# Attention ahead of two expert layers: plain float32 matmuls in place of split ones in the first 16 head units

## The chip, the cores and the metric
The kernel runs on one core of a Trainium2 chip. The core has TensorE for matmuls (the profile lists its weight loads as PEld beside PE), VectorE (DVE), ScalarE (ACT), GpSimd (POOL) and SyncE (SP), whose queue issues the DMAs here. The metric is the device time of one execution in microseconds; lower is better.

## The reference
Causal attention with a bias goes over 4 batches of 8 heads, 576 positions and 64 channels; its output feeds a gated layer and that one a second layer.

```python
scores = scale * np.matmul(q, k.transpose(0, 1, 3, 2))
cum = np.cumsum(np.maximum(s, 0.0), axis=-1)
bias = -(cum[:, :, :, None] - cum[:, :, None, :])
scores = np.where(causal, -1000000000.0, scores + np.minimum(bias, 0.0))
scores = scores - np.max(scores, axis=-1, keepdims=True)
attn = np.exp(scores)
attn = attn / (np.sum(attn, axis=-1, keepdims=True) + 1e-09)
out = np.matmul(attn, v)
# x: (2304, 512)
x = (1.0 / (1.0 + np.exp(-(x @ w_gate))) * (x @ w_val)) @ w_out
h = x @ w_in
y = (h - np.tanh(h)) @ w_out2
```

The weights and inputs are float32; w_gate and w_val are 512 by 1536.

## The kernel before
Matmuls use a reduced float32 type (called R in the code, fp32r in the profile). To keep float32 accuracy, each operand is split into a high part (a copy into R by ScalarE) and a low part (the difference, by GpSimd or VectorE), and products of the parts are summed in PSUM.

The attention works in head units of one batch, one head and one half G of the queries. The order is all units with G = 0 (queries 0 to 255, query tiles t = 0 and 1), 32 of them, and then those with G = 1 (tiles 2, 3, 4). Each unit has one step per tile, so the first 16 units are steps 0 to 31. An iteration i of the main loop handles several steps at once, as a pipeline written out by hand: `ttr(i)` adds scores and the broadcast cumulative sum and takes the row extreme (VectorE, L345); `exp(i)` is on ScalarE (L352); `eps`, `recip` and `norm` of step i-1 divide by the sum (VectorE, L356, L361, L370); `qk(i+1)` computes scores on TensorE (L331, L332); `tr(i-1)` transposes the probabilities through TensorE (L382); `evac(i-2)` copies them out of PSUM as high part (ScalarE, L395) and low part (VectorE, L396); `pv` multiplies by v when a unit's last tile is through (L409). `xsum` adds the two halves of the result (ScalarE copy L424, VectorE add L425), and `xsplit` splits the attention output of a pair of heads into high and low (ScalarE L433, GpSimd L434). Every engine runs its instructions in the order in which the code emits them.

For the scores, q is stored with its high part on partitions 0 to 63 and its low part on 64 to 127 (the input holds q and k twice, one below the other), so one matmul against the high part of k and one against its low part give all four products. `split_kq` makes these parts (ScalarE L284 and L288, GpSimd L285 and L289) and `split_v` those of v (ScalarE L302, GpSimd L303).

Loads are issued by SP in program order: `load_kq` two to three units ahead (L256), `load_vc` two units ahead (the broadcast rows of the cumulative sum, L268, and v, L270). Beside the attention, `Conversion.tick` prepares the 24 weight blocks of the gated layer, of 512 KB raw each, in three stages that overlap over ticks: a scaling on ScalarE (L74), a join on VectorE (L78, L79), the split (ScalarE L108, GpSimd L109). Three raw blocks are in flight; each tick issues the next load (L95). Two ticks (PRE) come ahead of the loop, then one in the iterations of `CS` (1, 3, ..., 13), then one in each from 15 on. When the eight heads of a batch and half are through, the loop hands out 24 groups of twelve expert matmuls each (`moe`, L456 to L460), two an iteration; the first are in iteration 20. The results go to DRAM (L442), and the two later stages follow after the attention.

Where the words end the code goes on:

Of the kernel before, what the change touches and what calls it, by code (L numbers as in the profile page):

```python
# [8 lines left out]
F = mybir.dt.float32  # L9
R = mybir.dt.float32r  # L10
U = mybir.dt.uint32
AF = mybir.ActivationFunctionType
ALU = mybir.AluOpType

B, H, S, D = 4, 8, 576, 64
# [11 lines left out]
NSP = 3  # L27
NK = 3
KA = 2
PRE = 2  # L30
CS = (1, 3, 5, 7, 9, 11, 13)
RAW0 = 2
AHEAD = 1
TR2 = 16
MP = M2 // 2
# [11 lines left out]
def width(t):  # L47
    return Q0[t] + 128
# [11 lines left out]
def attention_moe_moe2(ctx: ExitStack, tc: tile.TileContext, kqT, v, s, wg, wv, wo, win, wo2, out):  # L60
    nc = tc.nc
    PE, ACT, DVE, POOL, SP = nc.tensor, nc.scalar, nc.vector, nc.gpsimd, nc.sync
# [6 lines left out]
    def bank(i, shape):  # L69
        return psum.tile(shape, F, tag=f"bank{i}", name=f"bank{i}")  # L70
# [158 lines left out]
    ld = a_right.enter_context(tc.tile_pool(name="ld", bufs=2, side="right"))  # L229
    at = a_right.enter_context(tc.tile_pool(name="at", bufs=2, side="right"))  # L230
# [3 lines left out]
    make_identity(nc, ident)  # L234
    NPT = 1
    pts = [[pt.tile([128, 5, 320], R, name=f"pt{p}{i}") for p in "hl"] for i in range(NPT)]
    for st in pts:
        for p in st:
            POOL.memset(p.bitcast(F), 0.0)

    units = [(b, G, h) for G in range(2) for b in range(B) for h in range(H)]
    steps = [(u, t) for u, (b, G, h) in enumerate(units) for t in GRP[G][2]]
    U_ = {}

    def shape(u):
        b, G, h = units[u]
        q0, qw, ts = GRP[G]
        return b, h, q0, q0 + qw, qw, 2 if G == 0 else 5

    def load_kq(u):  # L250
        if u >= len(units):
            return
        b, h, q0, kw, qw, nj = shape(u)
        d = U_[u] = {}
        kq = ld.tile([128, S + 320], F, tag="kq", name="kq")[:, :kw + qw]
        SP.dma_start(out=kq, in_=kqT[b, h, :, 0:512] if q0 == 0 else kqT[b, h, :, 256:1152])  # L256
        d["q"], d["k"] = (kq[:, 0:256], kq[:, 256:512]) if q0 == 0 else (kq[:, S:], kq[:, :S])

    def load_vc(u):
        if u >= len(units):  # L260
            return
        b, h, q0, kw, qw, nj = shape(u)
        d = U_[u]
        d["v"] = ld.tile([128, 5, D], F, tag="v", name="vraw")[:, :nj]
        d["c"] = c = ld.tile([128, CW], F, tag="c", name="cbc", bufs=3)
        for t in GRP[units[u][1]][2]:
            k0 = 288 if t == 4 else 0
            SP.dma_start(out=c[:, CO[t]:CO[t] + width(t) - k0],  # L268
                         in_=cscr[b * H + h, k0:width(t)].partition_broadcast(128))
        SP.dma_start(out=d["v"], in_=v[b, h, :, 0:nj])  # L270

    parts, vparts = [], []

    def split_kq(u):
        if u >= len(units):
            return
        b, h, q0, kw, qw, nj = shape(u)
        d = U_[u]
        d["kh"] = kh = at.tile([128, S], R, tag="kh", name="kh", bufs=NK)[:, :kw]
        d["kl"] = kl = at.tile([128, S], R, tag="kl", name="kl", bufs=NK)[:, :kw]  # L280
        d["qs"] = qs = at.tile([128, 320], R, tag="qs", name="qs", bufs=NK)[:, :qw]

        def part_k():
            ACT.activation(out=kh, in_=d["k"], func=AF.Copy)  # L284
            POOL.tensor_tensor(out=kl, in0=d["k"], in1=kh.bitcast(F), op=ALU.subtract)  # L285

        def part_q():
            ACT.activation(out=qs, in_=d["q"], func=AF.Copy)  # L288
            POOL.tensor_tensor(out=qs[64:128], in0=d["q"][64:128], in1=qs[64:128].bitcast(F), op=ALU.subtract)  # L289

        parts.extend([part_k, part_q])

    def split_v(u):
        if u >= len(units):
            return
        b, h, q0, kw, qw, nj = shape(u)
        d = U_[u]
        d["vs"] = vs = at.tile([128, 5, 2, D], R, tag="vs", name="vs")[:, :nj]
        a = h % 2

        def part_v():
            ACT.activation(out=vs[:, :, a, :], in_=d["v"], func=AF.Copy)  # L302
            POOL.tensor_tensor(out=vs[:, :, 1 - a, :], in0=d["v"], in1=vs[:, :, a, :].bitcast(F), op=ALU.subtract)  # L303

        vparts.append(part_v)

    T_ = {}
    nqk = [0]
# [9 lines left out]
    def qk(i):  # L318
        if i >= len(steps):
            return  # L320
        u, t = steps[i]
        d = U_[u]
        q0 = GRP[units[u][1]][0]
        o = Q0[t] - q0
        w = width(t)
        cuts = [(0, max(w, 256))] if t < 4 else [(0, 288), (288, 576)]
        T_[i] = {"qk": []}
        for c0, c1 in cuts:
            ps = bank(3 + nqk[0] % 3, [128, c1 - c0])
            nqk[0] += 1  # L330
            PE.matmul(ps, d["qs"][:, o:o + 128], d["kh"][:, c0:c1], start=True, stop=False)  # L331
            PE.matmul(ps, d["qs"][:, o:o + 128], d["kl"][:, c0:c1], start=False, stop=True)  # L332
            T_[i]["qk"].append((ps, c0, min(c1, w)))
# [51 lines left out]
    def evac(i):  # L385
        if i < 0 or i >= len(steps):
            return
        u, t = steps[i]
        G = units[u][1]
        e = T_.pop(i)  # L390
        n = e["n"]
        ph, pl = pts[u % NPT]
        o = Q0[t] - GRP[G][0] + (64 if t == 4 else 0)
        js = slice(0, t + 1) if G else slice(0, 3 * t + 1, 3)
        ACT.activation(out=ph[:, js, o:o + n], in_=e["tr"], func=AF.Copy)  # L395
        DVE.tensor_tensor(out=pl[:, js, o:o + n], in0=e["tr"], in1=ph[:, js, o:o + n].bitcast(F), op=ALU.subtract)  # L396

    X_ = {}

    def pv(u):  # L400
        b, G, h = units[u]
        q0, qw, ts = GRP[G]
        d = U_.pop(u)
        ph, pl = pts[u % NPT]
        ps = bank(7, [128, qw])
        jobs = [(0, 0, 0), (1, 3, 0)] if G == 0 else [(0, 0, 0), (1, 1, 0), (2, 2, 0), (3, 3, 64), (4, 4, 64)]
        for n, (j, slot, o) in enumerate(jobs):
            for m, p in enumerate((ph, pl)):
                PE.matmul(ps[:, o:qw], d["vs"][:, j].rearrange("p a d -> p (a d)"), p[:, slot, o:qw],  # L409
                          start=(n == 0 and m == 0), stop=(n == len(jobs) - 1 and m == 1))  # L410
        return ps

    def xsum(u, ps):
        b, G, h = units[u]
        q0, qw, ts = GRP[G]
        g = 2 * b + G
        if h == 0:
            X_[g] = [xt.tile([128, KD, 320], R, tag=f"x{p}", name=f"x{p}")[:, :, :qw] for p in "hl"]
        a = 64 * (h % 2)
        if h % 2 == 0:  # L420
            X_["pair"] = at.tile([128, 320], F, tag="xp", name="xp", bufs=1)[:, :qw]
        xp = X_["pair"]
        tmp = at.tile([128, 320], F, tag="xtmp", name="xtmp", bufs=1)[:, :qw]
        ACT.activation(out=tmp[a:a + 64], in_=ps[64 - a:128 - a], func=AF.Copy)  # L424
        DVE.tensor_tensor(out=xp[a:a + 64], in0=ps[a:a + 64], in1=tmp[a:a + 64], op=ALU.add)  # L425

    def xsplit(u):
        b, G, h = units[u]
        g = 2 * b + G
        xp = X_["pair"]  # L430
        if h % 2:
            xh, xl = X_[g]
            ACT.activation(out=xh[:, h // 2, :], in_=xp, func=AF.Copy)  # L433
            POOL.tensor_tensor(out=xl[:, h // 2, :], in0=xp, in1=xh[:, h // 2, :].bitcast(F), op=ALU.subtract)  # L434
# [45 lines left out]
    load_kq(0)  # L480
    cvt = Conversion(cv, cq, 3, 3, RAW0)
    zt = at.tile([32, S], F, tag="sp", name="zt", bufs=NSP)
# [5 lines left out]
    load_vc(0)  # L488
    load_kq(1)
    load_vc(1)  # L490
    split_kq(0)
    while parts:
        parts.pop(0)()
    for _ in range(PRE):
        cvt.tick()
    mask(0)
    mask(1)
    split_v(0)
    split_kq(1)
    while parts:  # L500
        parts.pop(0)()
    vparts.pop(0)()
    load_kq(KA)
    qk(0)
    mq = []
    n = len(steps)
    xq, xs = [], []
    for i in range(n + LN + 1):
        u, t = steps[i] if i < n else (None, None)
        b, G, h = units[u] if i < n else (None, None, None)  # L510
# [3 lines left out]
        k = -(-len(mq) // left) if i < n else 0  # L514
        left -= 1
        for mm in mq[:k]:
            cvt.finish(min(2 * mm[1] + mm[2] + AHEAD, len(cq) - 1))
        eps(i - LN)
# [17 lines left out]
        while xq:  # L536
            xu, ps = xq.pop(0)
            xsum(xu, ps)
            xs.append(xu)
        if first:  # L540
            if vparts:
                vparts.pop(0)()
            split_kq(u + KA)
            split_v(u + 1)
            load_kq(u + KA + 1)
            load_vc(u + 2)
        for _ in range(2 if first and G == 0 else 1):
            if parts:
# [6 lines left out]
        e = i - LN - 1  # L555
# [5 lines left out]
            moe(*mq.pop(0))  # L561
        if CONV_AT(i):
            cvt.tick()
    for x in xq:
        xsum(*x)
        xsplit(x[0])
# [207 lines left out]
    op = ctx.enter_context(tc.tile_pool(name="op", bufs=1, side="left"))  # L774
# [37 lines left out]
    for i, (s, p) in enumerate(dsteps):  # L812
# [6 lines left out]
        w = WO[p]  # L819
        for n in OORD:  # L820
            g, f = OG[n], OW[n]
            for t in range(nt):
                o = acc[n][:, t * 256:t * 256 + 256]
# [52 lines left out]
```

## Time and profile before
| | |
|---|---|
| median of three runs | 1106.42 us (1104.88 to 1107.47) |
| profiled execution | 1104.14 us, span 1102.4 us, mean granted clock 0.996 |
| TensorE matmul / weight load busy | 1037.8 us (94%) / 1015.6 us (92%) |
| VectorE, ScalarE, GpSimd busy | 700.5, 561.9, 498.9 us |
| DMA | 182.49 MB, mean 166 GB/s |

The span runs from the first to the last instruction; busy times are unions on one engine, so they say nothing about which engine others wait for. The share of TensorE is an average over the whole kernel; in the page's 40 slices its tenths begin 2, 6, 6, 8, 8 and are nine almost everywhere after that.

### The profile page before, as it was taken

The numbers are of one execution on the slowest core, as the hardware profiler recorded it, in microseconds if no ns is written. First come the engines' busy times: TensorE is split into PE (matmuls) and PEld (weight loads), VectorE is DVE, ScalarE is ACT, GpSimd is POOL, SyncE is SP. The second block draws the span as 40 slices with busy tenths as digits, with TensorE's granted clock in tenths as the row PEclk, the third lists the DMA queues.
The fourth block names the chain that finished last, engine by engine and source line by source line (L and its number), as shares of the span: only waits on it lengthen the run. The fifth ranks groups of instructions, "written<-read, shape, count | busy, mean of one in ns | idle before, by whom it ended". The sixth has DMA issues, their size and how long they took to land.

```text
span 1102.4 us, 22100 instructions
## 1 busy us (share of the span) xinstructions
PE 1037.8 (94%) x7528; PEld 1015.6 (92%) x7528; DVE 700.5 (64%) x1686; ACT 561.9 (51%) x1342; POOL 498.9 (45%) x636
## 2 busy tenths in 40 slices
PE   2668899999999999999999999999999999999998
PEld 1468899899899999998999999999999999999998
DVE  5999756678777677663735654245444446778876
ACT  4866655667666566653534443344444433434332
POOL 6988644667666566651412211023333323254452
PEclk9999999999999999999999999999999999999999
DMA  5767444768465546531755553143455669644433
GB/s 190 233 205 226 109 119 142 204 146 181 149 168 145 167 132 167 165 88 43 259 176 182 170 185 103 58 150 134 157 209 202 259 223 348 225 121 137 145 90 111
DMA packets 122865, 182.49 MB, mean 166 GB/s; under 512 B 12864, under 2 KB 100416, under 8 KB 121472
## 3 DMA queue, kind: packets, MB, share of 16 engines
q1 hardware_dynamic: 122752, 181.08, 53.9%
q8 instruction: 59, 0.97, 0.4%
q14 instruction: 54, 0.44, 0.1%
HBM read 134.03 MB, written 47.00 MB: 164 GB/s over the span
## 4 chain that ended last, share of the span: by engine, by line
PE 84%; DVE 5%; DMA 4%; issue 3%; ACT 2%; POOL 1%; SPq 0%; DVEq 0%; POOLq 0%; ACTq 0%
PE bank L456 8%; PE bank L460 8%; PE bank L457 8%; PE bank L692 6%; PE bank L695 6%; PE bank L691 6%; PE bank L827 6%; PE bank L826 5%; PE bank L825 5%; PE bank L409 5%; PE bank L653 5%; PE bank L657 5%; PE bank L654 5%; PE bank L382 4%; PE bank L331 2%
## 5 line engine op out<-in xcount | busy, mean ns | idle before, releaser
L395 ACT ACTIVATE pth<-bank 128x320 fp32r<-128x320 f32 (+2 forms) x160 | 69.7, 435 | 147.4 <-PE bank L409 88.6
L827 PE MATMUL bank<-wo,sl 128*128 128x256 f32 x504 | 142.6, 283 | 0.0
L825 PE MATMUL bank<-wo,sh 128*128 128x256 f32 x504 | 141.8, 281 | 0.0
L826 PE MATMUL bank<-wo,sh 128*128 128x256 f32 x504 | 141.8, 281 | 0.0
L691 PE MATMUL bank<-yh,big 128*128 128x288 f32 x512 | 139.6, 294 | 0.0
L692 PE MATMUL bank<-yh,big 128*128 128x288 f32 x512 | 139.5, 295 | 0.0
L698 DVE TENSOR_TENSOR th<-bank,th 128x288 f32<-128x288 f32 x128 | 57.3, 456 | 114.3 <-ACT th L697 112.6
L382 PE MATMUL bank<-ident,sp 128*128 128x128 f32 (+1 forms) x480 | 78.1, 272 | 44.6 <-DVE ptl L396 20.9
L396 DVE TENSOR_TENSOR ptl<-bank,pth 128x320 fp32r<-128x320 f32 (+2 forms) x160 | 77.7, 486 | 66.5 <-PE bank L409 34.3
L382 PEld LDWEIGHTS bank<-ident,sp 128*128 128x128 f32 (+1 forms) x480 | 52.6, 143 | 60.0 <-DVE ptl L396 19.7
L697 ACT ACTIVATE th<-bank 128x288 f32<-128x288 f32 x128 | 51.8, 409 | 101.0 <-PE bank L695 99.3
L352 ACT ACTIVATE sp<-sp,nm 128x576 f32<-128x576 f32 (+2 forms) x160 | 95.6, 598 | 10.3 <-DVE nm L345 9.9
L827 PEld LDWEIGHTS bank<-wo,sl 128*128 128x128 f32 x504 | 95.3, 189 | 1.0 <-DVE sl L742 0.3
L692 PEld LDWEIGHTS bank<-yh,big 128*128 128x128 f32 x512 | 96.1, 188 | 0.0
L691 PEld LDWEIGHTS bank<-yh,big 128*128 128x128 f32 x512 | 96.0, 188 | 0.0
L826 PEld LDWEIGHTS bank<-wo,sh 128*128 128x128 f32 x504 | 95.3, 189 | 0.0
L825 PEld LDWEIGHTS bank<-wo,sh 128*128 128x128 f32 x504 | 95.3, 189 | 0.0
L735 POOL TENSOR_TENSOR s<-g 128x256 f32<-128x256 f32 (+1 forms) x40 | 35.4, 886 | 127.1 <-DMA g<-h 112.4
L695 PE MATMUL bank<-yl,big 128*128 128x288 f32 x512 | 88.6, 294 | 0.0
L599 DVE TENSOR_TENSOR gl<-g,gh 128x384 fp32r<-128x384 f32 x72 | 39.8, 556 | 76.4 <-PE bank L657 46.1
L303 POOL TENSOR_TENSOR vs<-vraw,vs 128x128 fp32r<-128x128 f32 (+1 forms) x64 | 44.5, 695 | 96.0 <-ACT vs L302 93.5
L370 DVE TENSOR_SCALAR sp<-sp,r 128x128 f32<-128x128 f32 (+1 forms) x96 | 85.1, 886 | 3.4
(351 smaller groups left out, 3253.8 us busy)
## 6 DMA issues: line engine op xcount, KB each, us to landing
h<-th SPq DMA_DIRECT2D x128, 144.0 KB, 2.4
kq<-in_kq SPq DMA_DIRECT2D x32, 448.0 KB, 3.8
raw<-in_wo SPq DMA_DIRECT2D x28, 512.0 KB, 4.9
g<-g SPq DMA_DIRECT2D x72, 192.0 KB, 2.8
g<-h SPq DMA_DIRECT2D x72, 128.0 KB, 2.3
w<-wst SPq DMA_DIRECT2D x5, 1792.0 KB, 6.5
wo<-w SPq DMA_DIRECT2D x5, 1792.0 KB, 8.3
kq<-in_kq SPq DMA_DIRECT2D x32, 256.0 KB, 3.8
```

The lines of the kernel that those rows point to most:

```text
L352: ACT.activation(out=e["sp"], in_=e["sp"], func=AF.Exp, scale=-1.0, bias=e["m"], accum_out=e["sum"])
L370: DVE.tensor_scalar(out=e["sp"], in0=e["sp"], scalar1=e["r"], scalar2=None, op0=ALU.mult)
L382: PE.transpose(ps[:, j, :], e["sp"][p0:128, c:c + 128], ident[p0:128, p0:128])
L456: PE.matmul(ps, wh[:, c], xh[:, k], start=(k == 0), stop=False)
L457: PE.matmul(ps, wl[:, c], xh[:, k], start=False, stop=False)
L460: PE.matmul(ps, wh[:, c], xl[:, k], start=False, stop=(k == KD - 1))
L691: PE.matmul(ps, wh[:, c], Y_[blk][k][0], start=(k == 0), stop=False)
L692: PE.matmul(ps, wl[:, c], Y_[blk][k][0], start=False, stop=False)
L695: PE.matmul(ps, wh[:, c], Y_[blk][k][1], start=False, stop=(k == KD - 1))
L825: PE.matmul(o, sh[:, g, c], w[:, 0, f], start=(p == 0 and t == 0), stop=False)
L826: PE.matmul(o, sh[:, g, c], w[:, 1, f], start=False, stop=False)
L827: PE.matmul(o, sl[:, g, c], w[:, 0, f], start=False, stop=(p == MP - 1 and t == nt - 1))
```

## The change
In the first 16 head units (`N32 = 16`: G = 0, batches 0 and 1) q and k are loaded once, on 64 partitions, and not split. Scores come from one float32 matmul a step, of 128 columns for tile 0 and 256 for tile 1. The transposed probabilities are copied out of PSUM by ScalarE alone, into a float32 tile of three blocks. v is loaded for two heads side by side, by the even unit of a pair, and one float32 matmul for each block of keys gives the values; the result has both heads' rows, of which a unit uses its own 64. `xsum` makes the high part from PSUM on ScalarE and the low part from PSUM on VectorE, and `xsplit` does nothing for these units. A third conversion tick stands ahead of the loop, the splits ahead of the loop go, the load of q and k comes two units ahead instead of three, and the two memsets of the probability tiles move from the start to the ends of iterations 30 and 31, still on GpSimd.

```diff
-PRE = 2
+PRE = 3
+N32 = 16
...
-    for st in pts:
-        for p in st:
-            POOL.memset(p.bitcast(F), 0.0)
...
+        if u < N32:
+            kq = at.tile([64, 512], F, tag="kh", name="kq32", bufs=NK)
+            SP.dma_start(out=kq, in_=kqT[b, h, 0:64, 0:512])
+            d["q"], d["k"] = kq[:, 0:256], kq[:, 256:512]
+            return
...
-        d["v"] = ld.tile([128, 5, D], F, tag="v", name="vraw")[:, :nj]
+        if u >= N32:
+            d["v"] = ld.tile([128, 5, D], F, tag="v", name="vraw")[:, :nj]
+        elif h % 2:
+            d["v"] = U_[u - 1]["v"]
+        else:
+            d["v"] = ld.tile([128, 2, 2, D], F, tag="v", name="vpair")
...
-        SP.dma_start(out=d["v"], in_=v[b, h, :, 0:nj])
+        if u >= N32:
+            SP.dma_start(out=d["v"], in_=v[b, h, :, 0:nj])
+        elif h % 2 == 0:
+            for a in range(2):
+                SP.dma_start(out=d["v"][:, :, a], in_=v[b, h + a, :, 0:nj])
...
     def split_kq(u):
-        if u >= len(units):
+        if u < N32 or u >= len(units):
             return
...
     def split_v(u):
-        if u >= len(units):
+        if u < N32 or u >= len(units):
             return
...
+        if u < N32:
+            ps = bank(3 + nqk[0] % 3, [128, w])
+            nqk[0] += 1
+            PE.matmul(ps, d["q"][:, o:o + 128], d["k"][:, 0:w], start=True, stop=True)
+            T_[i] = {"qk": [(ps, 0, w)]}
+            return
...
+        if u < N32:
+            if t == 0:
+                U_[u]["p"] = at.tile([128, 3, 128], F, tag="vs", name="p32")
+            ACT.activation(out=U_[u]["p"][:, t:2 * t + 1], in_=e["tr"], func=AF.Copy)
+            return
...
+        ps = bank(7, [128, qw])
+        if u < N32:
+            for j in range(2):
+                PE.matmul(ps[:, j * 128:], d["v"][:, j].rearrange("p a d -> p (a d)"),
+                          d["p"][:, 2 * j:2].rearrange("p s q -> p (s q)") if j == 0 else d["p"][:, 2],
+                          start=(j == 0), stop=(j == 1))
+            return ps
...
+        if u < N32:
+            xh, xl = (x[a:a + 64, h // 2, :] for x in X_[g])
+            ACT.activation(out=xh, in_=ps[a:a + 64], func=AF.Copy)
+            DVE.tensor_tensor(out=xl, in0=ps[a:a + 64], in1=xh.bitcast(F), op=ALU.subtract)
+            return
...
-        xp = X_["pair"]
-        if h % 2:
+        if u >= N32 and h % 2:
+            xp = X_["pair"]
...
-    split_kq(0)
-    while parts:
-        parts.pop(0)()
     for _ in range(PRE):
         cvt.tick()
     mask(0)
     mask(1)
-    split_v(0)
-    split_kq(1)
-    while parts:
-        parts.pop(0)()
-    vparts.pop(0)()
-    load_kq(KA)
     qk(0)
...
-            load_kq(u + KA + 1)
+            if u + KA < N32:
+                load_kq(u + KA)
+            if u + KA + 1 >= N32:
+                load_kq(u + KA + 1)
             load_vc(u + 2)
...
+        if i in (N32 - 2, N32 - 1):
+            POOL.memset(pts[0][i % 2].bitcast(F), 0.0)
```

## Rows read from the trace of the kernel before
**Rows 1.** Busy time by stretch (start:end, length, engines in turn, clock, DMA share, GB/s).

```profile
19.80:53.20 33.40, 19.37 (x77) 15.92 (x77) 31.62 (x104) 28.68 (x88) 31.78 (x47) 1.00 0.74 224
53.20:69.80 16.60, 6.66 (x28) 5.54 (x28) 14.88 (x35) 10.71 (x31) 14.76 (x18) 1.00 0.71 238
69.80:116.20 46.40, 39.08 (x311) 38.06 (x310) 42.63 (x111) 32.23 (x94) 37.68 (x44) 1.00 0.64 190
116.20:130.00 13.80, 12.88 (x96) 12.68 (x96) 10.40 (x43) 9.40 (x34) 9.64 (x18) 0.88 0.45 131
130.00:510.00 380.00, 370.00 (x2758) 356.17 (x2757) 263.07 (x853) 235.85 (x637) 221.85 (x338) 1.00 0.55 147
```

**Rows 2.** Timeline of VectorE: first instruction of iterations 2, 16, 20, 32 (start, duration).

```profile
19.78 0.15 DVE L356 TENSOR_SCALAR sum<-sum 128x1 f32<-128x1 f32 x1 [2.86 <-ACT sp L352]
...
53.23 0.15 DVE L356 TENSOR_SCALAR sum<-sum 128x1 f32<-128x1 f32 x1
...
69.82 0.14 DVE L356 TENSOR_SCALAR sum<-sum 128x1 f32<-128x1 f32 x1
...
116.22 0.14 DVE L356 TENSOR_SCALAR sum<-sum 128x1 f32<-128x1 f32 x1
```

**Rows 3.** Chain of waits, 103 to 108 us (start, length, what).

```profile
104.88 4.48 DMA raw<-in_wv
```

**Rows 4.** Waits of the DMA-issuing queue, 0 to 116.2 us (total, times, longest).

```profile
SPq L270 <- POOL vs L303: 36.1, 15, 4.8
```

**Rows 5.** Groups of VectorE by shape, 20 to 69 us (busy us, mean ns, idle before).

```profile
L370 DVE TENSOR_SCALAR sp<-sp,r 128x256 f32<-128x256 f32 x9 | 7.2, 803 | 0.3
L370 DVE TENSOR_SCALAR sp<-sp,r 128x128 f32<-128x128 f32 x9 | 4.8, 528 | 0.3
...
L396 DVE TENSOR_TENSOR ptl<-bank,pth 128x256 fp32r<-128x256 f32 x9 | 3.7, 415 | 0.0
...
L396 DVE TENSOR_TENSOR ptl<-bank,pth 128x128 fp32r<-128x128 f32 x9 | 2.5, 280 | 0.8 <-ACT pth L395 0.8
```

**Rows 6.** Timeline of VectorE, the same operation twice, 53 to 75 us.

```profile
65.69 1.38 DVE L370 TENSOR_SCALAR sp<-sp,r 128x128 f32<-128x128 f32 x1
...
73.33 0.29 DVE L370 TENSOR_SCALAR sp<-sp,r 128x128 f32<-128x128 f32 x1
```

**Rows 7.** Groups of GpSimd by shape, 20 to 69 us.

```profile
L289 POOL TENSOR_TENSOR qs<-kq,qs 64x256 fp32r<-64x256 f32 x10 | 7.7, 775 | 0.8
...
L285 POOL TENSOR_TENSOR kl<-kq,kh 128x256 fp32r<-128x256 f32 x9 | 6.7, 747 | 0.0
L303 POOL TENSOR_TENSOR vs<-vraw,vs 128x128 fp32r<-128x128 f32 x9 | 4.6, 507 | 2.0 <-ACT vs L302 1.9
L434 POOL TENSOR_TENSOR xl<-xp,xh 128x256 fp32r<-128x256 f32 x4 | 4.1, 1032 | 0.0
```

**Rows 8.** Chain of waits at 70 and at 127 us: matmuls and transposes (start, length).

```profile
70.28 0.21 PE bank L457
...
127.39 0.12 PE bank L457
...
127.99 0.22 PE bank L382 x2
```

**Rows 9.** Costliest groups of the page: weight load of a split matmul.

```profile
L825 PEld LDWEIGHTS bank<-wo,sh 128*128 128x128 f32 x504 | 95.3, 189 | 0.0
```

**Rows 10.** Timeline of ScalarE, 14 to 20 us.

```profile
14.10 0.39 ACT L352 ACTIVATE sp<-sp,nm 128x128 f32<-128x128 f32 x1
...
18.54 0.42 ACT L284 ACTIVATE kh<-kq 128x256 fp32r<-128x256 f32 x1 [3.95 <-DMA kq<-in_kq]
...
19.16 0.49 ACT L352 ACTIVATE sp<-sp,nm 128x256 f32<-128x256 f32 x1
```

**Rows 11.** Timeline of the DMA-issuing queue: third raw weight block.

```profile
10.96 0.43 SPq L95 DMA_DIRECT2D raw<-in_wg  x1
```

**Rows 12.** DMA issues, 0 to 130 us (count, KB each, median us to landing).

```profile
raw<-in_wg SPq DMA_DIRECT2D x12, 512.0 KB, 4.6
```

More of the change, by code (lines that the diff above doesn't have):

```diff
@@ L403, in pv @@
         d = U_.pop(u)
+        ps = bank(7, [128, qw])
[5 more added lines that the diff above has]
+            return ps
         ph, pl = pts[u % NPT]
-        ps = bank(7, [128, qw])
         jobs = [(0, 0, 0), (1, 3, 0)] if G == 0 else [(0, 0, 0), (1, 1, 0), (2, 2, 0), (3, 3, 64), (4, 4, 64)]
```

## The prediction
> **What bounds the kernel now.** I read the busy share by stretches first, cut at step starts found in VectorE's timeline: iteration 2 of the attention loop starts at 19.78, iteration 16 at 53.23, iteration 20 (the first with expert matmuls) at 69.82, iteration 32 (the first after the changed units) at 116.22 [rows 2]. From 130 to 510 us TensorE is busy 370 of 380 us [rows 1], and the page's slices stay at nine tenths nearly to the end, so a change ahead of it can only move that stretch earlier or later. Before 70 us it is different: between 19.8 and 53.2 TensorE is busy 19.4 of 33.4 us, VectorE and GpSimd 31.6 and 31.8, both 95% [rows 1]. Those two set the pace, 33.45 us for 14 steps, 2.39 us a step. From 53.2 to 69.8, where a weight conversion comes with every step, the four steps take 4.15 us each. From 69.8 to 116.2 the twelve steps take 3.87 us each with TensorE busy 39.1 of 46.4.
>
> Second, the chain of waits. In the stretch of expert matmuls it holds two pieces of about 4 us in which ScalarE waits for a raw weight block; one of them is shown [rows 3]. Why such a block is late is in the waits of the DMA-issuing queue: 36.1 us in 15 waits at L270, the load of v, for GpSimd's split of an earlier v (L303) [rows 4]. Everything behind that load in the queue, raw blocks among it, stands still meanwhile. So GpSimd's backlog is paid three times: by itself, by VectorE, whose shared operations stretch beside it, and by the queue.
>
> **What is removed, by unit (two steps).** VectorE loses the two L396 subtractions, 0.28 + 0.415 = 0.70 us [rows 5]; the add at L425 turns into a subtraction of the same size. GpSimd loses L285, L289, L303 and half an L434: 0.75 + 0.78 + 0.51 + 0.52 = 2.55 us [rows 7], of 4.55 (95% of two steps). VectorE's scaling by the reciprocal (L370) took 1.38 us at 65.69 and 0.29 at 73.33 in the same shape [rows 6]; means in the front are 0.53 (128 wide) and 0.80 (256 wide) [rows 5]. If 0.29 and some 0.40 (about L396's duration at that width) are the undisturbed values, 0.64 us of a unit is disturbance by GpSimd, and with GpSimd's load more than halved I take half of it back, 0.3 us. The GPSIMD Engine Reference of the Trainium skill (section 1, Specifications) says that GpSimd's SBUF interfaces are shared with VectorE, contended by its 2-port modes and two-input instructions; this trace agrees as far as the two durations of L370 go. ScalarE loses L284, L288, L302 and more; it was not the pace there (28.7 of 33.4), so I count nothing. The load of q and k halves from 256 to 128 KB (64 instead of 128 partitions of 2 KB).
>
> **What is added: plain float32 matmuls.** None is in this trace; the float32 transposes are another mode. The nearest rows are the split type's matmuls: 0.21 us for 256 columns while the engine is slack (so up to 72.8 us, the 1.2 GHz level by spacing, although the granted share reads 1.00), 0.12 us later, the 2.4 GHz level; two transposes take 0.22 there [rows 8]. A unit now has eight matmuls of 256 columns (0.95 us) and three transposes (0.33): 1.28 us, 0.64 a step. It gets four plain ones: 128 and 256 columns for scores, 256 and 128 for values. Below: they cost by columns like the others, 0.36 us, so 0.35 a step with transposes. Above: each has to be done in four parts by columns, with a weight load of 0.19 [rows 9] outside the matmul in each part: 4 x 4 x 0.19 = 3.0, and 3 x 4 x 0.12 = 1.4, with transposes 4.8 us, 2.4 a step. I take four parts with the loads hidden: (128 + 256 + 256 + 128) columns x 4 parts at 0.12 per 256 are 1.43, with transposes 1.77 a unit, 0.88 a step. Four parts, because the split form spends two full passes of doubled rows on the same products; loads hidden, because split matmuls follow each other every 0.12 us although a load lasts 0.19. The FP8 and Floating Point Precision page of the Trainium skill (TensorE Precision Notes) says that true FP32 takes four passes of the array; by that rule the sum is the one I took, and no row here shows it. At the slack level the same work is 2 x 1.28 + 0.64 = 3.2 us a unit.
>
> **The sum, stretch by stretch.**
> Start. Exp of step 0 runs at 14.1 now, and exp of step 1 only at 19.16, since ScalarE stands from 14.6 to 18.54 for the q and k of unit 2 (L284) [rows 10]. That copy goes. Instead the third conversion tick, now ahead of the loop, puts the scaling of the third raw block before exp of step 0. That block is issued at 10.96 [rows 11] and lands 4.6 us later [rows 12]: 15.6, scaling, exp and its read end at about 16.9, step 1 follows (minimum 0.5, exp 0.7): iteration 2 at 18.2. Gain 1.6; from 0, if the block comes later, to 3.
> Iterations 2 to 16. VectorE's 4.54 us a unit fall by 0.70 and 0.3 to 3.54, plus the 0.24 of idle time it has now: 3.8 us, 1.9 a step. Two others come close: TensorE at 3.2 plus any exposed load, and DMA, which now moves 224 GB/s at a 0.74 share [rows 1] and has 896 KB a unit left (one raw block 512, q and k 128, the two broadcasts 192, v 64): at a full share 303 GB/s, 3.0 us. I take 1.93. Gain 14 x 0.46 = 6.4. Bounds: 1.65 a step (VectorE freed of all disturbance, 4.54 - 0.70 - 0.64 a unit and a little idle time), 2.25 (TensorE's 3.2 a unit with its four loads exposed, at the slack level some 0.33 each, an estimate from the 0.19): gains of 10.4 and 2.0.
> Iterations 16 to 20. A unit has two conversions, 1.4 MB with the second raw block; at 238 to 303 GB/s that is 5.9 to 4.6 us, and VectorE has 3.5 + 1.5. I take 2.9 a step against 4.15, since the queue no longer waits for GpSimd at every unit. Gain 5.0, bounds 2 and 7.
> Iterations 20 to 32. 24 expert groups of twelve matmuls are 12 x 0.119 = 1.43 us each, 2.85 a step; with attention now 0.64, so 3.49, and 0.38 a step is lost to late blocks and VectorE. With 0.88 it is 3.73, and 0.2 of the loss I leave: 3.93 against 3.87. Loss 0.7; bounds a gain of 4 (0.35 a step, 0.34 lost) and a loss of 5 (four loads of 0.19 exposed once each: 1.26 a step).
> The new hidden work: two memsets of 1.4 us on GpSimd at iterations 30 and 31, which has a freed 2.5 us a unit there; without that cover the first old-style evacuation at iteration 33 would wait up to 2.9 us. The second v load of a pair and the extra tick lie on the queue and on engines that wait for the start anyway. From iteration 32 on nothing differs, and the four steps there without expert work [rows 1] stay as they are.
> Sum: 1.6 + 6.4 + 5.0 - 0.7 = 12.3 us, off the profiled 1104.1 (span 1102.4 and 1.7 around it): 1091.8. That execution is 2.3 us under the median of 1106.4; I forecast 1092.
>
> **The new wait.** The pair of v is held until the values matmuls of the older pair's second unit have run, so in every even unit the load of v stands in the queue until TensorE has passed them, one to one and a half steps later; the next raw block, the stores of expert results and the next q and k are behind it. That is six waits (two pairs are free at first) in place of fifteen. Two steps of prefetch in raw blocks cover it as long as a step is over some 2.5 us.
>
> **Rivals.**
> A. As summed: 1083 to 1099, chance 0.65.
> B. The queue stays the pace: six waits of up to one and a half steps (3 us early, 6 us late) are up to 27 us against 36, so late blocks remain and iterations 16 to 32 give nothing; only start and front do: 1104 - 7 = 1097, or less where the front also feels it, 1097 to 1102. For it: L270 is the largest wait of the queue now. Against: it comes half as often. Chance 0.13.
> C. Slower: plain matmuls cost the upper price. Iterations 20 to 32 then take 2.85 + 2.4 = 5.25 a step, 63 us against 46.4, a loss of 16.6; the front runs at 2.4 a step, as now; start and 16 to 20 give 6. Sum 1104 + 10 = 1114. It decides from where attention costs TensorE about 2.0 us a step, 3.9 a unit. Against: the loads hide behind the matmuls now [rows 8, 9]. Chance 0.10.
> D. Everything freed at once: 3 + 10 + 7 + 4 = 24 us, 1080. It needs VectorE undisturbed and one-part matmuls; chance 0.09.
> E. No change: gains of the front are given back in the stretch 20 to 32 (4.8 a step), 1102 to 1106, chance 0.03.
>
> **Numbers.** What this kernel can tell from no change is about 0.2%, 2.2 us. Faster: A, D, nearly all of B, 0.86; same: E and a little of B, 0.04; slower: C, 0.10. The range 1082 to 1101 takes A, most of B and a part of D.
>
> **What would show it.** Right: iteration 20's start near 57, iteration 32's near 104, the chain of waits without pieces of 4 us for raw blocks, L370 of 128 columns mostly near 0.3, GpSimd about half busy in the front, plain matmuls of 256 columns about 0.48 apart at the higher level. Wrong: plain matmuls above 0.9 us each among expert matmuls; VectorE still 95% busy at 2.3 us a step; waits of the queue at the v load summing to 30 us again; a gap at iterations 32 to 34 that was not there.

## The result: slower, and the profile after

The changed kernel took 1119.28 us (median of 4 runs, 1117.55 to 1120.33) against 1105.65 for the kernel before on the same chip (4 runs, 1104.55 to 1107.47): ratio 1.012, 95% interval 1.01 to 1.014. The forecast was 1092 and faster. The profiled execution's span is 1117.8 us (1102.4 before). "The new kernel" below is this one.

VectorE's timeline gives the starts of iterations 2, 16, 20 and 32, as in [rows 2] (the instruction's line is now L374):

```profile
21.14 0.15 DVE L374 TENSOR_SCALAR sum<-sum 128x1 f32<-128x1 f32 x1
...
54.40 0.15 DVE L374 TENSOR_SCALAR sum<-sum 128x1 f32<-128x1 f32 x1
...
74.11 0.15 DVE L374 TENSOR_SCALAR sum<-sum 128x1 f32<-128x1 f32 x1
...
130.39 0.15 DVE L374 TENSOR_SCALAR sum<-sum 128x1 f32<-128x1 f32 x1 [0.38 <-ACT sp L370]
```

Against [rows 2], iteration 2 is 1.4 us late, 16 is 1.2 late, 20 is 4.3 late and 32 is 14.2 late. So nearly all of the loss arises between iterations 16 and 32, and the front, where 6.4 us were to be gained, gains 0.2. The busy times by stretch, cut at these starts (columns as in [rows 1]):

```profile
21.10:54.40 33.30, 28.31 (x75) 17.10 (x75) 24.98 (x91) 20.04 (x62) 14.73 (x23) 1.00 0.58 175
54.40:74.10 19.70, 8.92 (x24) 5.21 (x23) 12.43 (x31) 8.43 (x23) 8.26 (x10) 1.00 0.51 166
74.10:130.40 56.30, 50.99 (x320) 45.01 (x319) 36.18 (x98) 27.44 (x78) 24.54 (x27) 0.94 0.51 150
```

The work was taken away: in the front VectorE fell from 31.6 to 25.0 us and GpSimd from 31.8 to 14.7. But in no stretch is VectorE, GpSimd or the DMA near its limit any more (the DMA share of the front fell too, from 0.74 to 0.58), and TensorE stands for 5 us in each of the three, or more: something waits. The waits of the DMA-issuing queue, 0 to 140 us (total, times, longest), say where. They answer to [rows 4]:

```profile
SPq L282 <- PE bank L430: 35.1, 6, 10.1
SPq L96 <- DVE tmp L80: 9.9, 4, 5.2
```

The 36.1 us in 15 waits of a v load for GpSimd became 35.1 us in 6 waits of a v pair's load for the values matmuls (L430) that still read the buffer. The sum is the same, but the time is 14 us worse. ScalarE's waits for raw weight blocks grew from 12.9 us in 7 (kernel before, 20 to 116 us) to 32.6 us in 11 (20 to 130 us); most are in this row of its waits:

```profile
ACT tmp L75 <- DMA raw<-in_wg: 24.7, 6, 8.6
```

The chain of waits from 50 to 70 us shows why (start, length, what):

```profile
52.87 7.39 DMA raw<-in_wv
...
60.34 0.66 ACT tmp L75
61.01 0.28 ACT p L413
61.29 0.04 issue
61.33 1.66 PE bank L430 x4
62.99 0.02 issue
63.01 0.38 SPq L282
...
64.01 3.91 DMA raw<-in_wg
...
68.01 0.66 ACT tmp L75
68.67 0.17 ACT p L413
```

It is a ring. ScalarE wants to scale a raw weight block (L75) and stands until the block is there. Behind that scaling in ScalarE's order is the copy of the transposed probabilities (L413); behind it, on TensorE, the values matmuls (L430); these free the v pair for which the queue has stood at L282; and behind L282 in the queue is the next raw block. ScalarE then stands for that one. ScalarE's timeline has the two waits in brackets:

```profile
60.34 0.66 ACT L75 ACTIVATE tmp<-raw 128x512 f32<-128x512 f32 x1 [3.32 <-DMA raw<-in_wv]
...
68.01 0.66 ACT L75 ACTIVATE tmp<-raw 128x512 f32<-128x512 f32 x1 [5.73 <-DMA raw<-in_wg]
```

Busy times between the two (the last columns are DMA share and GB/s): from 62 to 64 us nothing is moved, and what holds the next block back is its place in the queue.

```profile
60.00:62.00 2.00, 1.11 (x3) 0.76 (x4) 0.93 (x2) 1.66 (x5) 0.15 (x1) 1.00 0.04 14
62.00:64.00 2.00, 2.00 (x6) 1.08 (x4) 1.74 (x6) 0.28 (x1) 1.56 (x2) 1.00 0.00 0
```

One point of the description is corrected here. `N32` counts units, so the two memsets stand at the ends of iterations 14 and 15, not 30 and 31. They ran at 51.37 and 55.55 us, 1.43 us each on GpSimd; the 2.27 us of VectorE's scaling at 54.87 are beside one of them. What they cost was not measured alone.

### The profile page after: what moved, and what is told of

It reads as the page before. It is cut to its first block, busy times and chain, and to the rows that moved or that the text cites. A ratio compares the mean times of both kernels' runs of the same rounds, so it can differ in the third digit from the quotient of the medians.

```text
span 1117.8 us, 21882 instructions
## 1 busy us (share of the span) xinstructions
PE 1061.5 (95%) x7528; PEld 1023.6 (92%) x7528; DVE 681.7 (61%) x1654; ACT 546.0 (49%) x1286; POOL 458.7 (41%) x580
## 4 chain that ended last, share of the span: by engine, by line
PE 84%; DMA 6%; DVE 4%; ACT 2%; issue 2%; SPq 1%; POOL 0%; DVEq 0%; ACTq 0%; POOLq 0%
PE bank L490 8%; PE bank L491 8%; PE bank L494 8%; PE bank L722 6%; PE bank L725 6%; PE bank L721 6%; PE bank L857 5%; PE bank L855 5%; PE bank L856 5%; PE bank L438 5%; PE bank L683 4%; PE bank L684 4%; PE bank L687 4%; PE bank L400 4%; PE bank L349 2%; DMA raw<-in_wv 2%
## 5 line engine op out<-in xcount | busy, mean ns | idle before, releaser
L418 ACT ACTIVATE pth<-bank 128x512 fp32r<-128x512 f32 (+2 forms) x128 | 59.5, 465 | 144.0 <-PE bank L438 86.7
L419 DVE TENSOR_TENSOR ptl<-bank,pth 128x512 fp32r<-128x512 f32 (+2 forms) x128 | 66.7, 521 | 66.5 <-PE bank L438 39.2
L388 DVE TENSOR_SCALAR sp<-sp,r 128x128 f32<-128x128 f32 (+1 forms) x96 | 81.2, 845 | 3.4
L363 DVE CUSTOM_DVE_ANT_0 sp<-bank,cbc 128x288 f32<-128x288 f32 (+2 forms) x160 | 76.1, 476 | 4.2 <-POOL cbc L327 2.6
```

The costliest lines, as they stand in the source:

```text
L388: DVE.tensor_scalar(out=e["sp"], in0=e["sp"], scalar1=e["r"], scalar2=None, op0=ALU.mult)
```

## The experiments

Times are medians with the ratio to the kernel before on the same chip and its 95% interval. "Starts" are those of iterations 2, 16, 20 and 32, as above. Unless another kernel is named, an edit is made to the new kernel.

**1. A third buffer for the v pairs.** The first seven pairs take turns in the three buffers of the split q, which the plain units leave unused; the eighth has a buffer of v's own.

```diff
+            vp, tag, k = (at, "qs", NK) if u < 14 else (ld, "v", 2)
-            d["v"] = ld.tile([128, 2, 2, D], F, tag="v", name="vpair")
+            d["v"] = vp.tile([128, 2, 2, D], F, tag=tag, name="vpair", bufs=k)
```

> The changed kernel with three buffers in turn for the pairs of v instead of two (the first seven pairs lie in the three buffers of the split q, which these units leave free; the eighth stays in v's own). Theory 1, the load of a pair waits in the DMA-issuing queue for the values matmuls of an older pair, and the raw weight blocks behind it come late: the six waits at that load, 35.1 us together, go, iteration 20 starts near 61 us instead of 74 and iteration 32 near 109 instead of 130; time near 1097 us, ratio to the kernel before 0.985 to 0.997. Theory 2, the price of plain matmuls on TensorE makes the loss: the waits go too, but the time stays over 1112 us, ratio 1.005 to 1.014. Theory 3, the third conversion tick ahead of the loop makes it: as theory 2.

1097.14 us, ratio 0.9923 (0.9902 to 0.9944); starts 21.17, 50.03, 62.85, 108.59. The wait is gone from the queue, and 22 us come back: the buffer is the cause of the loss. Raw blocks now make ScalarE wait 3.9 us in all from 20 to 116 us.

**2. Two conversion ticks ahead of the loop, as before the change.**

```diff
-PRE = 3
+PRE = 2
```

> The changed kernel with two conversion ticks ahead of the loop as before, instead of three. Theory 1: the start gains 1 to 3 us (iteration 2 near 19 instead of 21.1), the waits at the load of the pair stay near 35 us, time 1115 to 1119 us. Theory 3, the tick sets the loss: below 1110 us. Theory 2 expects 1116 to 1119.

1122.06 us, ratio 1.0147 (1.0119 to 1.0175), slower than the 1115 to 1119 expected; starts 14.13, 50.27, 70.48, 133.63. The queue's wait for L430 is 35.5 us in 6. Iteration 2 starts 7.0 us earlier than in the new kernel, and by iteration 32 more than that is lost: with the ring in place, the tick doesn't decide.

**3. The kernel before, with a third buffer for v.** This asks whether [rows 4] was what set the time there.

```diff
-        d["v"] = ld.tile([128, 5, D], F, tag="v", name="vraw")[:, :nj]
+        if q0 == 0 and u % 3 == 2:
+            d["v"] = ld.tile([128, 2, D], F, tag="v0", name="vraw", bufs=1)
+        else:
+            d["v"] = ld.tile([128, 5, D], F, tag="v", name="vraw")[:, :nj]
```

> The kernel before with a third buffer in turn for v in the G = 0 units, nothing else. Theory 1 in its general form, a load of v that stands in the queue for a buffer makes raw weight blocks late: the waits of 36 us at L270 shrink to under 10, the pieces of 4 us for raw blocks in the chain go, 2 to 8 us faster than the kernel before. Rival, VectorE and GpSimd set the pace before 70 us whatever the queue does: within 2 us of the kernel before.

1105.23 us, ratio 1.0001 (0.9991 to 1.0011); starts 19.60, 53.05, 69.94, 114.63. The wait at the v load is gone, and the time stays. In this kernel's waits the q and k load (L256) waits for GpSimd instead (0 to 116 us; total, times, longest), and ScalarE's waits for raw blocks (20 to 116 us) fell from 12.9 us in 7 without a gain:

```profile
SPq L256 <- POOL qs L292: 19.7, 11, 3.0
```

```profile
ACT tmp L74 <- DMA raw<-in_wv: 4.9, 2, 3.6
```

So my reading that the queue's wait was a third payment for GpSimd's backlog falls. The load waited for an engine that was the pace anyway. A releaser that stands behind a raw block is not new by itself: in the kernel before, the timelines of ScalarE and of GpSimd have one too.

```profile
61.14 0.67 ACT L74 ACTIVATE tmp<-raw 128x512 f32<-128x512 f32 x1 [3.20 <-DMA raw<-in_wv]
```

```profile
63.17 0.46 POOL L303 TENSOR_TENSOR vs<-vraw,vs 128x128 fp32r<-128x128 f32 x1 [1.53 <-ACT vs L302]
```

Behind these the v load goes out at 63.66 and the next raw block at 64.08. Besides the pace, the lead differs, counted in the order of the code. Before, L303 stands in the same iteration as the load that it releases, and the raw block behind that load is scaled one step later; ScalarE waited 1.4 us for it. In the new kernel the values matmuls stand one iteration after the load. The pair's load of iteration 16 is released by the values matmuls of iteration 17 (61.33), the raw block queued behind it is the one that the tick of iteration 17 scales, and ScalarE waited for all of its landing, from 64.01 to 67.92.

**4. Both: third pair buffer and two ticks.** The edits of 1 and 2.

> The changed kernel with three buffers for the pairs of v and two ticks ahead of the loop. Theory 1: 1094 to 1097 us, 1 to 3 us under the version with three ticks, since exp of step 0 doesn't wait for the third raw block. Theory 2: over 1110 us. If the tick that comes later is missed at the start of the expert matmuls instead, it is equal to the version with three ticks.

1094.40 us, ratio 0.9894 (0.9868 to 0.992); starts 14.55, 46.35, 59.82, 107.96. It is faster than the kernel before, and the base of most runs below ("the mended kernel"). The largest of its queue's waits to 116 us, and its busy times by stretch:

```profile
SPq L96 <- DVE tmp L80: 14.0, 6, 4.4
```

```profile
14.50:46.40 31.90, 28.80 (x76) 17.50 (x76) 25.34 (x92) 20.16 (x63) 15.57 (x24) 1.00 0.76 234
46.40:59.80 13.40, 8.52 (x24) 5.15 (x23) 11.57 (x31) 8.29 (x23) 9.40 (x10) 1.00 0.73 223
59.80:108.00 48.20, 46.88 (x319) 41.91 (x317) 37.34 (x100) 29.21 (x79) 26.04 (x29) 1.00 0.67 189
```

TensorE is now the busiest engine of the front, 28.8 of 31.9 us.

**5. Plain matmuls in the first 8 units only**, on the mended kernel.

```diff
-N32 = 16
+N32 = 8
```

> The version with three buffers for the pairs of v and two ticks ahead of the loop, with plain matmuls only in the first 8 units (N32 = 8), so that the units beside expert matmuls are split again. Theory 2 in its smaller form, plain matmuls cost TensorE 0.3 us a step more beside expert work: iterations 20 to 32 fall from 48.1 us by up to 4 us, time 1090 to 1093 us. Rival, GpSimd's splits and the queue's wait for them come back there and take as much: 1093 to 1098 us.

1104.76 us, ratio 0.9993 (0.9983 to 1.0002); starts 14.29, 47.21, 69.68, 115.52. The time is above both expected ranges; the rival's mechanism is there, larger than priced: with the splits GpSimd's wait comes back, 27.9 us in 8 at the v load, and ScalarE waits 19.8 us for raw blocks. Iterations 16 to 20 take 22.5 us, so the 6.0 us gained by iteration 16 are gone by iteration 20. With eight plain units nothing is gained; as I read it, the gain of the mended kernel needs the splits gone while the conversions come with every step. What the change-over from plain to split units costs by itself was not separated.

**6. Two or four filler matmuls a step**, in iterations 4 to 19 of the mended kernel; nobody reads their result.

```diff
+        if 4 <= i < 20:
+            for _ in range(2):
+                PE.matmul(bank(0, [128, 256]), wgv[0][0][0][:, 0:128], wgv[0][0][0][:, 0:256], start=True, stop=True)
```

> The version with three buffers and two ticks, and in iterations 4 to 19 two idle matmuls of the split type and 256 columns a step, whose results nobody reads. In the version without them TensorE is busy 28.4 of 30 us in the front and yet its matmuls are spaced as at the 1.2 GHz level. Theory, the level follows the kind of matmul and plain ones don't raise it: plain matmuls of 256 columns go from 1.15 to about 0.63 us within a few steps, the front falls from 2.09 to 1.8 us a step, 2 to 5 us faster than without. Rival, the level has another cause: every step is 0.43 us longer, 5 to 8 us slower than without.

> The same with four idle matmuls a step. Theory: the 2.4 GHz level is reached if two were too few, time about that of the version without fillers or 2 to 4 us faster. Rival: 0.85 us a step longer, 10 to 15 us slower than without.

With two 1106.28 us, ratio 1.001 (1.0001 to 1.0019), with four 1125.75, 1.0189 (1.0171 to 1.0207). Both are slower than their expected ranges. Each filler writes the bank of the one before and waited for it (four took 2.50 us), so the runs only say that added time on TensorE's chain of the front is paid for the most part: from iteration 4 to 16 some 2.0 us a step with four fillers, which move the next matmul by 2.3 us.

**7. Four or eight fillers that add up into one bank without waiting**, the bank alternating between two. The edit for four:

```diff
+        if 4 <= i < 20:
+            ps = bank(i % 2, [128, 256])
+            for r in range(4):
+                PE.matmul(ps, wgv[0][0][0][:, 0:128], wgv[0][0][0][:, 0:256], start=(r == 0), stop=(r == 3))
```

> As the version with two idle matmuls a step, but four that accumulate in one bank, alternating over two banks, so that they run without waiting for one another (in the earlier versions each waited some 0.6 us for the one before it, so the engine was not dense). Theory, the level follows the kind of matmul: plain matmuls of 256 columns go from 1.15 to 0.63 us within some steps and the front is at most 0.1 us a step longer than without fillers, time 1090 to 1097 us. Rival, another cause: 0.85 us a step longer, 1104 to 1110 us.

> The same with eight accumulating idle matmuls a step. Theory: the level of 2.4 GHz holds through the front; 0.95 us a step of fillers stand against the faster plain matmuls, 1096 to 1106 us. Rival: 1.7 us a step longer, 1118 to 1126 us.

With four 1095.38 us, ratio 0.99 (0.9883 to 0.9918), with eight 1097.66, 0.9927 (0.991 to 0.9945): four cost nothing that shows. The scores of 256 columns in TensorE's timeline, first in the mended kernel, then with four fillers (start, duration; one plain matmul is recorded as two instructions, x2):

```profile
34.72 1.22 PE L342 MATMUL bank<-kq 64*128 64x256 f32 x2
```

```profile
35.31 0.70 PE L342 MATMUL bank<-kq 64*128 64x256 f32 x2
35.93 0.74 PE L583 MATMUL bank<-w00h 128*128 128x256 f32 x4
```

The same matmul takes 1.22 us at the 1.2 GHz spacing and 0.70 at that of 2.4. Iteration 16 starts at 46.33 against 46.35. TensorE is busy as long as before, now with the fillers (28.9 us of 31.5), but from 29 to 46 us the chain of waits holds no matmul: VectorE and two loads of the broadcast rows (4.1 and 3.7 us) are in it. So with TensorE's work faster, other work holds the front at about 2 us a step. Experiment 11 agrees: there TensorE is busy 20.0 us of the front's 30.7.

**8. The two loads of a pair later**, one iteration on and behind the raw block of that iteration in the queue, with the new kernel's two buffers and two ticks. `load_pair` holds the two loads.

```diff
-            for a in range(2):
-                SP.dma_start(out=d["v"][:, :, a], in_=v[b, h + a, :, 0:nj])
+            if u < 4:
+                load_pair(u)
+            else:
+                late.append(u)
...
+        if late and i % 2:
+            load_pair(late.pop(0))
```

> The changed kernel with two ticks ahead of the loop and its two buffers for the pairs of v, but from the third pair on the load is issued one iteration later, behind the values matmuls that free its buffer and behind that iteration's raw weight block. Theory 1, not the buffer but what stands in the queue behind the load makes the loss: the waits at the load of the pair fall under 10 us, time 1093 to 1100 us as with three buffers. Rival, the loads of v themselves are late: near 1120 us.

1106.10 us, ratio 1.0007 (0.9998 to 1.0017), where 1093 to 1100 was expected: a miss. The wait is shorter but not gone. The row of the queue's waits, here and (second fence) in experiment 2:

```profile
SPq L291 <- PE bank L439: 18.0, 6, 4.0
```

```profile
SPq L282 <- PE bank L430: 35.5, 6, 9.1
```

With experiment 4 they form a series with two ticks: 35.5 us of this wait give 1122.1, 18.0 give 1106.1, none gives 1094.4. What keeps half of the wait was not looked into.

**9. One values matmul instead of two**, on the mended kernel, to price a term; keys 128 to 255 are left out of the values.

```diff
-            for j in range(2):
+            for j in range(1):
...
-                          start=(j == 0), stop=(j == 1))
+                          start=True, stop=True)
```

> The version with three buffers and two ticks, which leaves out the second values matmul of each of the first 16 units (keys 128 to 255 of these queries). Theory 2 in its smaller form, TensorE at the slack level is the pace of the front: 0.5 us less a unit of 4.18 there and 0.25 beside expert matmuls, 3 to 6 us faster than with it. Rival, VectorE or DMA would hold the front at 4 us a unit: within 1.5 us.

1092.09 us, ratio 0.9879 (0.9863 to 0.9894); starts 14.76, 44.89, 57.91, 105.15. 2.3 us came back where 3 to 6 were expected, 1.5 of them by iteration 16: TensorE is only a part of the front's pace, as experiment 7 says too.

**10. The v pair as one load with rows of 1 KB**, from an input laid out by pairs, on the mended kernel.

```diff
+            SP.dma_start(out=d["v"], in_=v2[b, h // 2])
```

> The version with three buffers and two ticks, with v of the first 16 units laid out by pairs in the input, so that a pair is one load with 1 KB a partition instead of two loads in rows of 256 bytes. In the changed kernel and its mended versions raw weight blocks take 5.8 to 7.3 us to land, 4.1 to 4.5 before. Theory, the many small packets make them late: landing falls to near 4.5 us, iterations 16 to 20 shorten from 13.5 us, time 1089 to 1093 us. Rival, the loads are closer together in time and share the DMA engines: landing stays over 5.5 us and the time within 1.5 us of the version without.

1094.24 us, ratio 0.99 (0.9883 to 0.9918): no difference from 1094.40. Raw blocks of `in_wv` and `in_wg` took 6.3 and 5.8 us to land, 5.9 and 6.9 in the mended kernel. So the small rows of v are not what makes raw blocks land later than the 3.9 to 4.6 us of the kernel before.

**11. q and k on 128 partitions**, on the mended kernel, partitions 64 to 127 filled with zeros from an input.

```diff
-            kq = at.tile([64, 512], F, tag="kh", name="kq32", bufs=NK)
-            SP.dma_start(out=kq, in_=kqT[b, h, 0:64, 0:512])
+            kq = at.tile([128, 512], F, tag="kh", name="kq32", bufs=NK)
+            SP.dma_start(out=kq, in_=kq0[b, h])
```

> Three buffers for the v pairs and two ticks of preparation, as in the best version, and q and k of the plain units lie on 128 partitions, the lower 64 of which hold zeros, so the score matmuls run on 128 rows (the k and q load is twice as large, half of it zeros from an input). The question is a term of the sum: plain scores of 128 and 256 columns measured 0.42 and 0.63 us at the higher clock level against 0.21 and 0.43 for four parts, and the first expert matmul behind one took 0.31 against 0.12. Theory (the 64-row form among 128-row ones makes the extra): in iterations 20 to 32 scores of 256 columns take about 0.43, the matmul behind them 0.12, iterations 20 to 32 shorten from 48.2 to 44-46 us, and the time is 1089-1093 (the version with 64 rows: 1094.4). Rival (plain scores cost that on any number of rows): scores stay at 0.6, iterations 20 to 32 at 47.5 to 49, and the time is 1094-1098, the doubled load adding a little.

1091.27 us, ratio 0.9877 (0.986 to 0.9893), the lowest median of the versions that do all the work, though its interval overlaps that of experiment 4; starts 14.11, 44.83, 58.39, 104.13. Scores among expert matmuls in TensorE's timeline, with 64 rows (mended kernel) and with 128:

```profile
87.49 0.70 PE L342 MATMUL bank<-kq 64*128 64x256 f32 x2
88.11 0.39 PE L491 MATMUL bank<-xh,w06h 128*128 128x256 f32 x1
88.33 0.28 PE L492 MATMUL bank<-xh,w06l 128*128 128x256 f32 x1
```

```profile
67.33 0.59 PE L342 MATMUL bank<-kq 128*128 128x256 f32 x2
67.58 0.47 PE L491 MATMUL bank<-xh,w02h 128*128 128x256 f32 x1
67.88 0.28 PE L492 MATMUL bank<-xh,w02l 128*128 128x256 f32 x1
```

From the start of the scores to the start of the second expert matmul it is 0.84 us with 64 rows and 0.55 with 128, although both do the same columns. Four parts and one expert matmul make 5 x 0.12 = 0.60. So a float32 matmul costs four parts, and the rest came with the 64 rows. Iterations 20 to 32 shorten from 48.1 to 45.7 us, inside the 44 to 46 expected, but they took 45.7 in experiment 1 too, with 64 rows, so the length of this stretch doesn't show it; the spacing does.

## Why the prediction was wrong, by its steps

**The step that failed is "The new wait".** It saw the wait, its six times and what is queued behind it, and then covered it: "Two steps of prefetch in raw blocks cover it as long as a step is over some 2.5 us." It sized the wait in steps (one to one and a half) and took a step's length as given. But the release itself stands, by way of ScalarE's order, behind the arrival of a raw block, and the next raw block stands behind the wait; late blocks make long steps and long steps make late blocks. The two steps of prefetch were not there either. From iteration 15 on a tick comes with every step and queues the block of the next one, a lead of one step in the order of the code, and the release comes one step after the load: nothing is left, as the block of 64.01 shows (experiment 3). The six waits lasted 5.9 us each in the mean, up to 10.1. Experiments 1, 4 and 8 show it: the third buffer is 22 us faster with three ticks and 27.7 with two, and at half the wait somewhat under half of the loss is left. Of what should show it wrong, "waits of the queue at the v load summing to 30 us again" is what came.

**Rival B, the queue as the pace,** had the place right and the sign wrong. It priced the new wait by the old one (27 against 36 us), but experiment 3 shows that the old one cost nothing. A sum of waits is no price; who waits behind whom is.

Rivals D and E have no ring either and didn't come about. **Rival C,** the only one that ended slower, gave 1114, near the measured time by another mechanism, so by luck. It decides from 2.0 us a step of attention on TensorE. In the chain of waits of the new kernel, 94 to 107 us, among expert matmuls:

```profile
94.86 0.31 PE bank L490
95.17 0.12 PE bank L491
...
96.59 0.66 PE bank L430 x4
...
98.68 0.63 PE bank L341 x2
...
102.59 0.42 PE bank L341 x2
```

A unit is 0.66 for the values (384 columns), 0.63 and 0.42 for the scores, 0.33 for the transposes and twice 0.19 that the expert matmul behind scores takes beyond 0.12: 2.4 us, 1.2 a step. The forecast said 0.88, rival C 2.4. The values come out at the price taken (0.72); the scores were mis-sized, because they have 64 rows (experiment 11). The Trainium skill's FP8 and Floating Point Precision page (TensorE Precision Notes) says four passes for true FP32; the values, and the scores on 128 rows, agree. The TensorEngine Tiling (Array Packing) page of the Trainium skill (Key Properties) says that changing the tiling mode drains the engine; the extra that vanishes with 128 rows agrees with that, but no run here separates a drain from another cost of 64 rows.

**Start** (gain 1.6, measured a loss of 1.4). The third tick's scaling came at 18.11, not about 15.6, since the block was late, and exp of step 0 behind it at 18.68 in place of 14.10 [rows 10]. ScalarE's timeline of the new kernel:

```profile
18.11 0.66 ACT L75 ACTIVATE tmp<-raw 128x512 f32<-128x512 f32 x1 [9.82 <-DMA raw<-in_wg]
18.68 0.39 ACT L370 ACTIVATE sp<-sp,nm 128x128 f32<-128x128 f32 x1
```

With the third buffer, the median with two ticks is 2.7 us below that with three (1094.40 against 1097.14, intervals that overlap by a little).

**Iterations 2 to 16** (gain 6.4). With the ring 0.2; without it (experiment 1, 28.9 us) 4.6, inside the bounds of 2.0 to 10.4. The pace that I expected from VectorE, 3.8 us a unit, was for the most part TensorE's, 4.18 (values of successive units start at 24.20 and 28.38 in experiment 1): 1.29 for values, 1.15 and 0.72 for scores and 1.03 for transposes at the slack level, where 3.2 was taken. Of VectorE's relief, 0.3 us a unit in the sum, nothing came: GpSimd's load fell by half, and the scaling [rows 5] of 128 columns went from 0.528 to 0.353 us, but that of 256 from 0.803 to 1.116. VectorE by shape, 20 to 76 us of the new kernel:

```profile
L388 DVE TENSOR_SCALAR sp<-sp,r 128x256 f32<-128x256 f32 x10 | 11.2, 1116 | 0.4
...
L388 DVE TENSOR_SCALAR sp<-sp,r 128x128 f32<-128x128 f32 x10 | 3.5, 353 | 0.4
```

The trace shows what the wide ones met. A tick's split of a weight block (L110 on GpSimd, 1.3 us) was not taken away, and it falls into the step of the wide scaling; the timelines of VectorE and of GpSimd at one of them:

```profile
29.21 1.14 DVE L388 TENSOR_SCALAR sp<-sp,r 128x256 f32<-128x256 f32 x1
```

```profile
28.93 1.27 POOL L110 TENSOR_TENSOR w11l<-tmp,w11h 128x512 fp32r<-128x512 f32 x1 [2.37 <-ACT w11h L109]
```

Nine of the ten wide ones ran beside L110 and took 0.89 to 2.27 us; the tenth began before it and took 0.35. Nine of the ten narrow ones ran clear of it and took 0.29, and the one beside it took 0.95.

**Iterations 16 to 20** (gain 5.0): with the ring a loss of 3.1, without it a gain of 3.8. **Iterations 20 to 32** (loss 0.7): with the ring a loss of 9.9, without it a gain of 0.7.

So without the ring the four stretches sum to -1.4 + 4.6 + 3.8 + 0.7 = 7.7 us gained of 12.3 forecast, and 1097.1 lies in the forecast range: the removed work was worth a gain, and one buffer less than needed turned it into a loss. That says little for the single terms: the start had the wrong sign, the front was paced by another engine, and that iterations 20 to 32 gained although attention was dearer there is luck. The version of experiment 11 is 1.2% faster than the kernel before and, by the two ratios, some 2.4% faster than the new one.

## What to carry to other kernels

When a load stands in an in-order queue until a buffer is read, follow the release all the way back: if the reader stands, on any engine, behind data that is queued behind that same load, the wait feeds itself. Count, in the order of the code, the steps from the release to the use of what is queued behind the load: with one step, and other engines as the pace, the wait cost nothing here; with none it cost 22 to 28 us, at nearly the same sum. One more buffer is the test. When an operation is new to a trace, ask whether its shape is new too: here the kind was priced right and the 64 rows were not.

## What the runs showed of the hardware that was not expected

**TensorE's clock stayed at its lower level beside long busy times.** In the mended kernel TensorE is busy 28.8 of 31.9 us in the front and stays at the 1.2 GHz spacing until the expert matmuls (each 256-column score took 1.22 us), although its chain of waits holds nothing but TensorE from 28.9 to 44.9 us. Four split-type matmuls more a step brought the 2.4 GHz spacing (0.70, experiment 7), while two that waited for each other did not (1.22 still). With the scores on 128 rows and nothing added it rose as well, in places: TensorE's timeline of experiment 11 has the 256-column scores at both levels.

```profile
25.36 1.06 PE L342 MATMUL bank<-kq 128*128 128x256 f32 x2
...
29.51 0.60 PE L342 MATMUL bank<-kq 128*128 128x256 f32 x2
...
37.09 0.60 PE L342 MATMUL bank<-kq 128*128 128x256 f32 x2
...
45.20 1.06 PE L342 MATMUL bank<-kq 128*128 128x256 f32 x2
```

The granted clock in the record doesn't tell it here: it reads 1.00 over the mended kernel's front and 0.94 over that of experiment 11, which has the shorter spacings. What in the 128 rows raised the level was not separated, and how much of the front's 1.5 us came from it and how much from the scores' own price stays open.

**Raw blocks land later.** In the new kernel those of `in_wv` took 7.3 us from issue to landing between 20 and 60 us (3.9 before), with a lower DMA share, and 5.9 to 6.9 in the mended one. The size of v's rows is not the reason (experiment 10), and neither are the plain units: in experiment 3, which keeps every split and only takes the wait at the v load out of the queue, they took 6.0 us (`in_wv`) and 6.3 (`in_wg`) in the same stretch, against 3.9 and 4.4. In the new kernel, too, the blocks that go out right behind the pair's wait (`in_wg`) took 4.2. So a short landing goes with a pause in the queue just ahead of the block; that the loads ahead of it are then still being moved would explain it, but was not shown.
